# Near attention in 24-query, 32-key tiles, weights' low parts on three engines, and a new plan

## The chip, the cores and the metric

The kernel runs on one core of one Trainium2 chip. The metric is the device time of one execution in microseconds (us). The engines are TensorE (PE in the rows; its weight loads are PEld), VectorE (DVE), ScalarE (ACT), GpSimd (POOL) and SyncE (SP), which starts most transfers. Each engine works through its own list of instructions in a fixed order and waits on semaphores for what the others produce.

## The reference, cut to what matters

Three layers follow one another; q, k and v are 4 x 8 x 576 x 64 (batch, head, position, dimension).

```python
def _attn_ref(q, k, v):                        # factor = 4, Sd = 144, scale = 1/8
    q_d = q.reshape(B, H, Sd, factor, D).mean(axis=3)        # k_d, v_d alike
    ...
    out_up = np.repeat(sm_attn(q_d, k_d, v_d), factor, axis=2)      # far part
    mask = np.abs(pos[:, None] - pos[None, :]) < factor
    scores = np.where(mask, scale * np.matmul(q, k.transpose(0, 1, 3, 2)), -1e9)
    ...
    return out_up + np.matmul(attn, v)                        # near part

def _moe_ref(x, w1, w2, w3, w_out):            # x 2304 x 512, w1..w3 512 x 768
    h = np.maximum(np.maximum(x @ w1, x @ w2), x @ w3)
    return h @ w_out

def _moe2_ref(x, w_gate, w1, w2):              # 8 experts, each 512 -> 1024 -> 512
    expert_idx = np.argmax(x @ w_gate, axis=1)
    ...
        out[mask] = gate_w[mask, None] * (np.maximum(xe @ w1[e], 0.0) @ w2[e])
```

So each position attends to 144 averaged positions (far) and to the at most seven positions nearest to it (near).

## The kernel before, in words

**Attention** is worked in 16 pairs of heads, numbered u. For each pair q and k lie with two heads on 128 partitions and 576 positions along them.
- *Far part*: four neighbouring positions are summed (on VectorE by `sum4`, line 345, or on TensorE by matmuls with the identity, `tp`, line 354, which the flag "pp" chooses), scores `td` (459) are reduced, exponentiated and normalised, turned by `tu` (509), and multiplied with value sums. The value sums come from `sum4_v`, three GpSimd instructions (365 to 367).
- *Near part*: the 576 queries are cut into ten tiles of 58 queries; a tile needs 64 keys. `near` (378 to 390) puts a mask into two PSUM banks `ts` of five tiles each with matmuls (380, 382), then adds the scores with 20 matmuls per pair (389; the chip's list shows each run as two). VectorE takes the maximum per bank (399), subtracts it (405); ScalarE exponentiates; VectorE sums (433), inverts (437, 441) and normalises (445, or GpSimd with the flag "nn"). With the flag "nb" ScalarE does the subtraction and the sum by itself. Five transposes `tt` (493) into two banks turn the result, ScalarE copies it to `pt`.
- *Output*: `to` in two banks of 288 columns. A pair with the flag "pb" takes the wide way: the far part is spread over all 576 columns by six matmuls (534, run as twelve), and the near matmuls (548) add to it. The others have the far part in 144 columns, `tz` (520), and VectorE adds it to the near part while it spreads it, `x` (557). Then ScalarE rounds to a high part of `xb` (575), and VectorE or GpSimd takes the low part (577).

**The hidden layer.** Float32 products are made from high and low parts: high x high, high x low and low x high, 12 matmuls of 256 columns for one tile `hp` (929), 18 tiles and 216 matmuls for a block of 256 tokens; nine blocks. The three weight matrices come as 64-bit floating-point words in 18 blocks of 128 x 512. ScalarE takes the magnitude (702), VectorE narrows it to float32 with four instructions (`narrow`, 709 to 719), ScalarE rounds to the high part `wh` (724), GpSimd subtracts it for the low part `wl` (727). `w_out` is treated alike in 24 blocks of 128 x 128. The first block of tokens needs the outputs of the first four head pairs, and all of a block's 18 tiles need all 18 weight blocks.

**The order.** The kernel is scheduled by hand: a planner, `Plan`, holds every piece of work as a job with an engine, a cost, the jobs it waits for, the buffers it takes and gives back, and a wanted time. Among those of an engine that can start earliest, within 0.02 us, it takes the one whose wanted time is smallest:

```python
t0 = min(t for t, _ in c)
...
c = [x for x in c if x[0] <= t0 + (0.02)]
...
t, j = min(c, key=lambda x: (x[1]["want"], x[1]["n"]))
```

The wanted times come from tables of numbers (`BATCH`, `PAIR`, `STEP` for attention, `WEIGHTS`, `W_OUT`, `HIDDEN`, `ROWS`), the form of each pair from `FORMS`. Where the planner sees TensorE waiting it puts in `warm` matmuls (1835), whose result is read by nobody. PSUM has two tags of four banks: "at" for attention, "mm" for the hidden layer. The expert layer follows, planned by the same class.

Of the kernel before, what the change touches and what calls it, by code (L numbers as in the profile page):

```python
# [10 lines left out]
F32 = mybir.dt.float32  # L11
F32R = mybir.dt.float32r
# [22 lines left out]
WIN, KW = 58, 64  # L35
NW = 10
CUT = (0, S // 2, S)
NEG = -8.0e9
# [3 lines left out]
    "fn sq xl",  # L42
    "fn nn pb sk xl",
    "fn pb pp sq",
    "fn nb nn sq xl",
    "nb pb",
    "fn nn sk xl",
    "nb pb pp sk sq",
    "nb pp sq",
    "",  # L50
    "pp sq",
    "nn",
    "nn pp sq",
    "fn nn pp xl",
    "nb sk sq xl",
    "nn sk",
    "fn nb sq",
# [3 lines left out]
BATCH, PAIR, STEP = (-274.5, 218.0, 224.5, 310.0), 14.0, (38.4, -2.5, 82.2, 8.0, -10.4, 1.3, -5.5, -32.1, 50.8, -98.4)  # L61
WEIGHTS, W_OUT = (-61.6, -163.2, -24.2, -102.5, 169.6, 33.5), (-204.54, 5.46)
HIDDEN, ROWS, RESTS = (1322.17, 50.07, -176.85), (908.92, -14.66), 10.0
# [11 lines left out]
def queries(w):  # L75

    g, i = divmod(w, NW // 2)
    return g * S // 2 + i * WIN, min(WIN, S // 2 - i * WIN)


def first_key(w):

    return min(max(queries(w)[0] - 3, 0), S - KW)


def _consts():
# [18 lines left out]
    mask = np.zeros((2, 64, 3, KW))  # L105
    for i, w in enumerate((0, 1, NW - 1)):
        q = queries(w)[0] + np.arange(WIN)
        k = first_key(w) + np.arange(KW)
        mask[:, 0:WIN, i] = np.where(np.abs(q[:, None] - k[None, :]) < 4, 0.0, NEG)
# [163 lines left out]
class Attention:  # L273
# [5 lines left out]
    def __init__(s, nc, pool, psum, q, k, v, vs, C, block):  # L279
# [4 lines left out]
        s.vb = [pool.tile([128, NW // 2, 2, D], F32, name=f"vb{i}") for i in range(s.VB)]  # L284

    def setup(s):
        nc, P = s.nc, s.pool
        s.ident16 = P.tile([128, 128], BF16, name="ident16")
        nc.scalar.copy(out=s.ident16, in_=s.C["ident"])
        s.mask16 = P.tile([128, 3, KW], BF16, name="mask16")  # L290

    def plan_mask(s, pl, mask):
        st = {}

        def load():
            st["m"] = s.tile("pt", [128, NW // 2, 128]).rearrange("p a b -> p (a b)")[:, 0:3 * KW]
            s.nc.sync.dma_start(out=st["m"], in_=mask)
# [30 lines left out]
    def load_vb(s, u):  # L328
# [3 lines left out]
        s.nc.sync.dma_start(out=s.st[u]["vb"].rearrange("p i h d -> p (i h d)"), in_=s.vs[b, hp])  # L332
# [29 lines left out]
    def sum4_v(s, u):  # L362

        nc, vr = s.nc, s.st[u]["vr"]
        nc.gpsimd.tensor_tensor(out=vr[:, :, 0:2], in0=vr[:, :, 0:2], in1=vr[:, :, 2:4], op=ALU.add)
# [1578 lines left out]
```

## Time and profile before

| what | value |
|---|---|
| three runs, us | 706.24, 707.4, 709.99 (median 707.4) |
| the profiled execution, us | 710.75 |
| its span on the core, us | 708.9 |
| mean granted TensorE clock | 0.988 of full speed |
| read from and written to device memory | 75.18 MB and 9.70 MB |

The span is the time from the first to the last recorded instruction; the profiled execution is 1.85 us longer. Busy shares are means over the whole span; attention and the weights fill its first part, the hidden layer and the experts the rest, so each stretch is read by itself. An instruction's duration can include what it waits for on a shared resource, so the shortest and the mean duration of one form are read side by side.

### The profile page before, as it was taken

The page shows a single profiled execution, that of the slowest core. Times are in us where ns is not written, and L with a number is a line of the kernel's source. Part 1 is how long each engine was busy: PE and PEld are TensorE (multiplying, and loading weights), DVE is VectorE, ACT ScalarE, POOL GpSimd, SP SyncE. Part 2 cuts the span into 40 slices and gives each one's busy share as a digit, 9 for nine tenths or more (in the row PEclk, how much of TensorE's full clock was granted, in tenths as well). Part 3 has the DMA queues.
Part 4 walks back from the last instruction along what each step waited for, and adds up shares of the span by engine and source line. Part 5 has one row for each costly group of instructions (what it writes and reads, how often), then busy time and mean ns, then how long its engine had stood idle before and what let it go on. Part 6 is the DMA issues. An engine that isn't in the chain of part 4 may idle for free. (4 is left out here: it accounts for less than half of the span.)

```text
span 708.9 us, 15595 instructions
## 1 busy us (share of the span) xinstructions
PE 684.8 (97%) x6145; PEld 605.4 (85%) x6155; DVE 359.6 (51%) x900; ACT 270.4 (38%) x781; POOL 167.5 (24%) x197
## 2 busy tenths in 40 slices
PE   9989799999999999999999999999999999999993
PEld 5655689889899999999999999889888788787772
DVE  3999998988543552242222228377121121148860
ACT  3655564666441552231111112341222222156850
POOL 3656664433630121110000000213211210201110
PEclk9999999999999999999999999999999999999997
DMA  8447442335330110101000001624534342535440
GB/s 287 140 152 249 153 137 78 109 116 159 115 122 13 33 52 5 44 1 48 17 16 16 16 31 58 202 91 153 183 113 156 132 136 90 187 126 172 169 142 28
DMA packets 34547, 75.24 MB, mean 106 GB/s; under 512 B 4575, under 2 KB 7903, under 8 KB 34464
## 3 DMA queue, kind: packets, MB, share of 16 engines
q1 hardware_dynamic: 28832, 59.73, 26.0%
q0 software_dynamic: 3040, 9.70, 4.2%
q10 hardware_dynamic: 2592, 4.72, 1.8%
q8 instruction: 50, 0.82, 0.5%
q14 instruction: 33, 0.27, 0.1%
HBM read 75.18 MB, written 9.70 MB: 120 GB/s over the span
## 5 line engine op out<-in xcount | busy, mean ns | idle before, releaser
L929 PE MATMUL hp<-xb,wh 128*128 128x256 f32 x1296 | 228.6, 280 | 0.1
L929 PEld LDWEIGHTS hp<-xb,wh 128*128 128x128 f32 x1296 | 196.8, 189 | 1.3 <-issue 0.6
L929 PE MATMUL hp<-xb,wl 128*128 128x256 f32 x648 | 179.9, 278 | 0.0
L929 PEld LDWEIGHTS hp<-xb,wl 128*128 128x128 f32 x648 | 122.1, 188 | 0.0
L939 DVE TENSOR_TENSOR hf<-hf,hp 128x256 f32<-128x256 f32 x108 | 45.2, 419 | 90.7 <-PE hp L929 88.4
L1499 PEld LDWEIGHTS ehp<-xT,ew 128*128 128x128 f32 x672 | 78.3, 188 | 3.6 <-ACT ob L1657 1.7
L1499 PE MATMUL ehp<-xT,ew 128*128 128x256 f32 x672 | 79.9, 280 | 0.0
L1513 DVE SCALAR_TENSOR_TENSOR ehT<-ehp,ehT 128x256 fp32r<-128x256 f32 x56 | 23.7, 424 | 107.4 <-ACT ehT L1511 107.3
L1523 PE MATMUL eo<-ew,ehT 128*128 128x512 f32 x336 | 78.2, 392 | 0.0
L1523 PEld LDWEIGHTS eo<-ew,ehT 128*128 128x128 f32 x336 | 62.5, 188 | 15.3 <-DVE xT L1598 0.8
L957 PE MATMUL yp<-woh,ht 128*128 128x260 f32 (+1 forms) x408 | 70.5, 292 | 0.0
L942 ACT CAST ht<-hf 128x256 fp32r<-128x256 f32 x54 | 21.9, 406 | 105.9 <-DVE hf L939 105.7
L1577 POOL DMA_INDIRECT xg<-y,r_go x14 | 14.5, 1036 | 187.3 <-DVE r_go L1115 120.7
L957 PEld LDWEIGHTS yp<-woh,ht 128*128 128x128 f32 x408 | 56.9, 188 | 1.8 <-issue 0.8
L1662 POOL DMA_INDIRECT out_dram<-ob,r_si x19 | 20.1, 1059 | 122.2 <-ACT ob L1657 102.9
L1568 DVE TENSOR_TENSOR ew<-wr,ew 128x1024 fp32r<-128x1024 f32 x36 | 42.9, 1221 | 11.6 <-ACT ew L1564 10.6
L1511 ACT ACTIVATE ehT<-ehp 128x256 fp32r<-128x256 f32 x56 | 21.5, 383 | 67.5 <-PE ehp L1499 67.4
L957 PE MATMUL yp<-wol,ht 128*128 128x260 f32 (+1 forms) x204 | 43.2, 288 | 0.0
L1564 ACT CAST ew<-wr 128x1024 fp32r<-128x1024 f32 x36 | 37.0, 1052 | 6.8 <-PE ehp L1607 2.6
L1835 PE MATMUL warm<-const-bfloat16-1.0 128*128 128x512 bf16 x123 | 33.1, 417 | 1.9 <-issue 0.8
L1657 ACT ACTIVATE ob<-eo,r_ga 128x512 f32<-128x512 f32 (+1 forms) x18 | 12.1, 676 | 58.7 <-PE eo L1523 29.4
L727 POOL TENSOR_TENSOR wl<-tmp,wh 128x512 fp32r<-128x512 f32 x18 | 27.4, 1524 | 24.7 <-ACT wh L724 24.6
(230 smaller groups left out, 1034.3 us busy)
## 6 DMA issues: line engine op xcount, KB each, us to landing
wr<-in_moe_w_dram SPq DMA_DIRECT2D x36, 512.0 KB
rw<-in_moe_w_dram SPq DMA_DIRECT2D x64, 256.0 KB
raw<-in_moe_w_dram SPq DMA_DIRECT2D x18, 512.0 KB
vb<-in_vs_dram SPq DMA_DIRECT2D x16, 320.0 KB
vr<-in_v_dram SPq DMA_DIRECT2D x16, 288.0 KB
qt<-in_q_dram SPq DMA_DIRECT2D x16, 288.0 KB
kt<-in_k_dram SPq DMA_DIRECT2D x16, 288.0 KB
y<-ys ACTq DMA_DIRECT2D x18, 256.0 KB
```

Of the source, the lines that this page charges most:

```text
L727: s.nc.gpsimd.tensor_tensor(out=lo, in0=t, in1=hi.bitcast(F32), op=ALU.subtract)
L929: s.nc.tensor.matmul(t, s.w[a][:, kk, g, m * 128:(m + 1) * 128], s.xb[j][:, x, kk], start=n == 0, stop=n == 11)
L939: s.nc.vector.tensor_tensor(out=s.hf[j, m], in0=s.hf[j, m], in1=s.hp.pop((j, m, g)), op=ALU.max)
L942: s.nc.scalar.copy(out=s.ht[j][:, 0, m], in_=s.hf[j, m])
L957: s.nc.tensor.matmul(p, s.ht[j][:, a, kk, ts], s.wo[w][:, kk, c0:c1], start=kk + i == 0, stop=kk + i == 7)
L1499: s.nc.tensor.matmul(t, s.W1[j][:, a, f * 128:(f + 1) * 128], s.xL[:, x, j], start=n == 0, stop=n == 11,)
L1511: nc.scalar.activation(out=h, in_=t, func=ACTF.Relu)
L1513: nc.vector.scalar_tensor_tensor(out=l, in0=t, scalar=0.0, in1=h.bitcast(F32), op0=ALU.max, op1=ALU.subtract,)
L1523: s.nc.tensor.matmul(s.op[k, 0], h[a][:, j, i * 128:(i + 1) * 128], s.W2[:, b, j], start=j == 0 and w == 0, stop=j == 7 and w == 2,)
L1564: s.nc.scalar.copy(out=h, in_=r)
L1568: (s.nc.gpsimd if eng == "Pool" else s.nc.vector).tensor_tensor(out=l, in0=r, in1=h.bitcast(F32), op=ALU.subtract)
L1835: nc.tensor.matmul(t, one(128), one(512), start=True, stop=True)
```

## The change

- **Near tiles.** 24 queries and 32 keys in place of 58 and 64. The positions are cut into four parts (`NP`) of six tiles. All scores of a pair stand in one bank of 128 x 3 x 4 x 32; they take 48 matmuls per pair (run as 96). One maximum, one subtraction and one sum for a pair, each over 384 columns; three transposes into one bank. The mask has three variants of 32 keys. Value rows for the near part grow from 320 to 384 KB per pair, as more tiles overlap.
- **Outputs.** Four banks of 144 columns in place of two of 288, taken by turns from the tags "at" and "mm"; 48 near matmuls of 24 columns (run as 96). `x` and `xb` come in four pieces in place of two.
- **Low parts of the weights.** A table, `LOW`, puts each on GpSimd, VectorE or TensorE: of 18 blocks nine, five and four, of the 24 of `w_out` eight, twelve and four. On TensorE the value times the identity, less the high part times the identity, go into a bank, and ScalarE copies it out.
- **Value sums.** A new flag "dv" puts the value sums on VectorE, in nine pairs of 16.
- **The plan.** New costs for the jobs (a `tp` job 2.08 in place of 0.99), new forms and new wanted times. Pairs that take the wide way: four before, five now; pairs that sum q and k on TensorE: six and six.

Lines have other numbers now: scores 393, maximum 403, subtraction 408, sum 435, transposes 494, outputs 538 and 550, `x` 559, `xb` 577 and 579, narrowing 707 to 717, low parts 725, 761 and 762, `hp` 942, `warm` 1849.

```diff
-WIN, KW = 58, 64
-NW = 10
-CUT = (0, S // 2, S)
+WIN, KW = 24, 32
+NP = 4
+NW = S // NP // WIN
+CUT = range(0, S + 1, S // NP)
...
 FORMS = (
-    "fn sq xl",
-    "fn nn pb sk xl",
...
+    "dv pb pp sq xl",
+    "fn nb nn sq",
...
+LOW = (
+    "Pool", "PE", "DVE", "PE", "Pool", "Pool",
...
-WEIGHTS, W_OUT = (-61.6, -163.2, -24.2, -102.5, 169.6, 33.5), (-204.54, 5.46)
+WEIGHTS, W_OUT = (-206.2, 90.3, 239.1, 628.7, 412.7, 434.6), (-1970.43, 64.68)
...
+        t = st["ts"] = s.bank([128, NW // 2, NP, KW], "ts")
+        x, n = t.rearrange("p a i k -> p (a i) k"), NW // 2 * NP
+        for i, (a, b) in enumerate(((0, 1), (1, n - 1), (n - 1, n))):
+            m = s.mask16[:, i:i + 1].to_broadcast([128, b - a, KW])
+            nc.tensor.matmul(x[:, a:b], s.ident16, m, start=i == 0, stop=False)
+        for w in range(0, NW, 2):
+            for i in range(NP):
+                for p in range(2):
+                    k, c = first_key(i, w + p), CUT[i] + (w + p) * WIN
+                    for h in range(2):
+                        r, o = slice(64 * h, 64 * h + 64), 64 * p + 32 * h
+                        nc.tensor.matmul(
+                            t[o:o + WIN, w // 2, i], st["q"][r, c:c + WIN], st["k"][r, k:k + KW],
+                            start=False, stop=w == NW - 2 and i == NP - 1,
+                        )
...
+    def out_bank(s, i):
+        return s.psum.tile([128, S // NP], F32, name="to", tag=("at", "mm")[i % 2], bufs=4)
...
+        for t in range(NW):
+            for i in range(NP):
                 for h in range(2):
-                    p = 64 * (h ^ g)
+                    r, c = slice(32 * i, 32 * i + 32), t % 2 * 64 + 32 * h
                     nc.tensor.matmul(
...
+                        st["to", i][64 * h:64 * h + 64, t * WIN:t * WIN + WIN], st["vb"][r, t, h],
+                        st["pt"][r, t // 2, c:c + WIN], start=alone, stop=alone or t == NW - 1,
...
-        add("sv", "Pool", 2.5, lambda: s.sum4_v(u), "lr", t=T[2])
+        sv = "DVE" if "dv" in flags else "Pool"
+        add("sv", sv, 1.25 if sv == "DVE" else 2.5, lambda: s.sum4_v(u, sv), "lr", t=T[2])
...
+        def less():
+            n = int(np.prod(st["v"].shape[1:]))
+            p = st["p"] = s.bank(n, "wlow")
+            s.nc.tensor.matmul(p, s.C["ident"], st["v"], start=True, stop=False)
+            s.nc.tensor.matmul(p, s.nid, hi(), start=False, stop=True)
+            vals.append(st["v"])
+
+        j = pl.add("PE", d[5], less, [j, more], want, get=("mm",), put=(tag + "t",))
+        return pl.add("ACT", d[6], lambda: s.nc.scalar.copy(
```

How instructions stand now, at three places. First VectorE (DVE), the start of its list before, where `qk` are sums of four, `smx` and `sm` the near part, `dmx` the far part:

```order
L345 TENSOR_REDUCE qk<-qt 128x144
L345 TENSOR_REDUCE qk<-kt 128x144
L399 TENSOR_REDUCE smx<-ts 128x5 x2
L468 TENSOR_REDUCE dmx<-td 72x2 x2
L472 TENSOR_SCALAR dmx<-dmx 72x2
L405 TENSOR_TENSOR sm<-ts,smx 128x5x64
```

The same start now, where `tmp` is a weight block being narrowed:

```order
L403 TENSOR_REDUCE smx<-ts 128x12
L408 TENSOR_TENSOR sm<-ts,smx 128x384
L707 TENSOR_SCALAR tmp<-tmp 128x512
L709 TENSOR_SCALAR tmp<-tmp 128x512
L435 TENSOR_REDUCE sms<-sm 128x12
L713 SCALAR_TENSOR_TENSOR tmp<-raw,tmp 128x512
L439 TENSOR_SCALAR sms<-sms 128x12
```

Sums of four have left the start of the list, and the weights stand third. Next VectorE around the two `x` instructions of the fourth head pair, before:

```order
L709 TENSOR_SCALAR tmp<-tmp 128x512
L437 TENSOR_SCALAR sms<-sms 128x10
L711 TENSOR_SCALAR tmp<-tmp 128x512
L441 RECIPROCAL sms<-sms 128x10
L715 SCALAR_TENSOR_TENSOR tmp<-raw,tmp 128x512
L557 TENSOR_TENSOR x<-to,dn 128x288 x2
```

Now, with that pair's `x` in a group of three and one more:

```order
L471 TENSOR_REDUCE dmx<-td 72x2 x2
L403 TENSOR_REDUCE smx<-ts 128x12
L408 TENSOR_TENSOR sm<-ts,smx 128x384
L709 TENSOR_SCALAR tmp<-tmp 128x512
L435 TENSOR_REDUCE sms<-sm 128x12
L559 TENSOR_TENSOR x<-to,dn 128x144 x3
L713 SCALAR_TENSOR_TENSOR tmp<-raw,tmp 128x512
L707 TENSOR_SCALAR tmp<-tmp 128x512
L471 TENSOR_REDUCE dmx<-td 72x2
L559 TENSOR_TENSOR x<-to,dn 128x144
```

Between the conversion steps the near part stands in single instructions for 12 tile rows (`smx` 128x12), and `x` in pieces of 144. Last, TensorE (PE) ahead of the first hidden matmul (`hp`), before, where `warm` rows between are left out:

```order
L520 MATMUL tz<-pd,vr 128x144 x3
L354 MATMUL tp<-qt,cs 128x144 x4
L354 MATMUL tp<-kt,cs 128x144 x4
L509 MATMUL tu<-cs,ds 96x72 x6
L459 MATMUL td<-qk 72x144 x4
L1835 LDWEIGHTS const-bfloat16-1.0
L1835 MATMUL warm<-const-bfloat16-1.0 128x512
...
L389 MATMUL ts<-kt,qt 58x64 x16
L389 MATMUL ts<-kt,qt 56x64 x4
L929 MATMUL hp<-xb,wh 128x256 x2
```

Now:

```order
L393 MATMUL ts<-kt,qt 24x32 x48
L761 MATMUL wlow<-tmp,cs 128x512
L762 MATMUL wlow<-wh,nid 128x512
L1849 LDWEIGHTS const-bfloat16-1.0
L1849 MATMUL warm<-const-bfloat16-1.0 128x512
L519 MATMUL tz<-pd,vr 128x144 x3
...
L550 MATMUL to<-pt,vb_79 64x24 x48
...
L462 MATMUL td<-qk 72x144 x4
...
L942 MATMUL hp<-xb,wh 128x256 x2
```

In the lists the pieces of attention ahead of `hp` are of the same kinds; the `warm` rows ahead of it number 114 before and 50 now, and the low part of a weight block (`wlow`) stands among them.

## Rows read from the trace of the kernel before

**Rows 1.** Page, part 1: busy time, share of the span, instructions
```profile
PE 684.8 (97%) x6145; PEld 605.4 (85%) x6155; DVE 359.6 (51%) x900; ACT 270.4 (38%) x781; POOL 167.5 (24%) x197
```

**Rows 2.** Windows: stretch; its us; busy us (instructions) by engine; granted clock; DMA share; GB/s
```profile
0.00:72.00 72.00, 65.53 (x661) 41.60 (x669) 56.56 (x125) 37.90 (x137) 40.17 (x48) 0.98 0.62 205
75.00:117.00 42.00, 38.93 (x390) 35.42 (x391) 37.76 (x81) 21.50 (x71) 23.20 (x19) 0.96 0.41 125
117.00:290.00 173.00, 171.82 (x2097) 162.87 (x2096) 104.28 (x345) 84.26 (x327) 54.24 (x78) 1.00 0.27 81
88.20:91.60 3.40, 3.40 (x51) 2.88 (x51) 3.40 (x13) 3.24 (x12) 2.40 (x3) 0.50 0.35 86
```

**Rows 3.** Groups on PE, 0 to 75: count, busy us, mean ns, idle before
```profile
L1835 PE MATMUL warm<-const-bfloat16-1.0 128*128 128x512 bf16 x106 | 28.9, 423 | 1.8 <-issue 0.8 <-PEq L1931 0.8 <-DVE sm L405 0.2
```

**Rows 4.** Timeline of PE: start us, us, work [idle before, releaser]
```profile
74.86 0.50 PE L929 MATMUL hp<-xb,wh 128*128 128x256 f32 x2
...
87.09 0.74 PE L493 MATMUL tt<-cs,sm 128*128 128x128 f32 x5 [2.72 <-DVE sm L445]
```

**Rows 5.** Groups on DVE, 0 to 72
```profile
L715 DVE SCALAR_TENSOR_TENSOR tmp<-raw,tmp 128x512 int32<-128x512 int32 x10 | 9.2, 915 | 0.1
L719 DVE SCALAR_TENSOR_TENSOR tmp<-raw,tmp 128x512 int32<-128x512 int32 x10 | 8.9, 887 | 0.1
L709 DVE TENSOR_SCALAR tmp<-tmp 128x512 f32<-128x512 f32 x10 | 7.1, 710 | 1.3 <-ACT tmp L702 1.1
L711 DVE TENSOR_SCALAR tmp<-tmp 128x512 int32<-128x512 int32 x10 | 5.4, 538 | 0.0
L399 DVE TENSOR_REDUCE smx<-ts 128x5 f32<-128x320 f32 x10 | 4.6, 480 | 0.8 <-PE ts L389 0.8
...
L433 DVE TENSOR_REDUCE sms<-sm 128x10 f32<-128x640 f32 x3 | 2.4, 812 | 0.1
...
L345 DVE TENSOR_REDUCE qk<-qt 128x144 f32<-128x576 f32 x3 | 2.2, 728 | 8.2 <-DMA qt<-in_q_dram 8.2
...
L577 DVE TENSOR_TENSOR xb<-to,xb 128x256 fp32r<-128x256 f32 (+3 forms) x8 | 1.9, 300 | 1.6 <-ACT xb L575 1.6
L557 DVE TENSOR_TENSOR x<-to,dn 128x288 f32<-128x288 f32 x4 | 1.6, 445 | 0.0
```

**Rows 6.** Lines 709 and 719: ns min/median/max, first and last start
```profile
L709 DVE TENSOR_SCALAR tmp<-tmp x18: 411/456/2285, 16.4 to 104.7; 128x512 f32<-128x512 f32 x18
...
L719 DVE SCALAR_TENSOR_TENSOR tmp<-raw,tmp x18: 675/684/1668, 30.1 to 107.1; 128x512 int32<-128x512 int32 x18
```

**Rows 7.** Groups on POOL, 0 to 72
```profile
L727 POOL TENSOR_TENSOR wl<-tmp,wh 128x512 fp32r<-128x512 f32 x9 | 13.7, 1525 | 13.6 <-ACT wh L724 13.6
L485 POOL TENSOR_TENSOR ds<-ds,dsu 72x288 f32<-72x288 f32 x8 | 6.0, 774 | 10.0 <-DVE dsu L441 9.0 <-DVE sms L437 1.0
L365 POOL TENSOR_TENSOR vr<-vr 96x384 f32<-96x384 f32 x4 | 4.4, 1092 | 5.1 <-DMA vr<-in_v_dram 4.9 <-PE ts L389 0.2
L367 POOL TENSOR_TENSOR vr<-vr,cs 96x384 f32<-96x384 f32 x4 | 3.6, 906 | 0.3
L366 POOL TENSOR_TENSOR vr<-vr 96x192 f32<-96x192 f32 x4 | 3.0, 750 | 0.3
```

**Rows 8.** Timeline of PE, pieces of attention between other work
```profile
74.14 0.79 PE L389 MATMUL ts<-kt,qt 64*58 64x64 f32 x40
...
92.28 3.07 PE L534 MATMUL to<-pd,vr 96*128 96x288 f32 x12
...
95.29 0.81 PE L548 MATMUL to<-pt,vb 64*64 64x58 f32 x40
...
99.24 0.71 PE L493 MATMUL tt<-cs,sm 128*128 128x128 f32 x5
```

**Rows 9.** Windows of line 389 alone, within its piece at 74.14
```profile
74.13:74.16 0.03, 0.02 (x4) 0.03 (x4) 1.00 1.32 546
74.16:74.23 0.07, 0.07 (x4) 0.07 (x8) 1.00 0.85 351
```

More of the change, by code (lines that the diff above doesn't have):

```diff
@@ L103, in _consts @@
     }
[L105 to L109, printed above, removed]
+    mask = np.zeros((2, 2, 32, 3, KW))
+    for n, (i, t) in enumerate(((0, 0), (0, 2), (NP - 1, NW - 2))):
+        for j in range(2):
+            q = CUT[i] + (t + j) * WIN + np.arange(WIN)
+            k = first_key(i, t + j) + np.arange(KW)
+            mask[j, :, 0:WIN, n] = np.where(np.abs(q[:, None] - k[None, :]) < 4, 0.0, NEG)
     c["mask"] = mask.reshape(128, -1)
@@ L283, in __init__ @@
         s.st = {u: {} for u in range(s.n)}
-        s.vb = [pool.tile([128, NW // 2, 2, D], F32, name=f"vb{i}") for i in range(s.VB)]
+        s.vb = [pool.tile([128, NW, 2, D], F32, name=f"vb{i}") for i in range(s.VB)]
     def setup(s):
@@ L485, in far_norm, with turn_near, take_near @@
         s.on(on).tensor_tensor(out=x, in0=x, in1=r.to_broadcast([72, 2, 3, 48]), op=ALU.mult)
-    def turn_near(s, u, g):
+    def turn_near(s, u):
         nc, st = s.nc, s.st[u]
-        a, b = ((0, 3), (3, NW // 2))[g]
-        t = st["tt", g] = s.bank([128, b - a, 128], "tt")
-        for i in range(a, b):
-            x = st["sm"][:, i].rearrange("p g k -> p (g k)")
-            nc.tensor.transpose(t[:, i - a], x, s.C["ident"])
-    def take_near(s, u, g):
+        t = st["tt"] = s.bank([128, NW // 2, 128], "tt")
+        for a in range(NW // 2):
+            nc.tensor.transpose(t[:, a], st["sm"][:, a].rearrange("p i k -> p (i k)"), s.C["ident"])
+    def take_near(s, u):
         st = s.st[u]
-        a, b = ((0, 3), (3, NW // 2))[g]
-        if g == 0:
-            st["pt"] = s.tile("pt", [128, NW // 2, 128])
-        s.nc.scalar.copy(out=st["pt"][:, a:b], in_=st.pop(("tt", g)))
+        st["pt"] = s.tile("pt", [128, NW // 2, 128])
+        s.nc.scalar.copy(out=st["pt"], in_=st.pop("tt"))
     def turn_far(s, u):
@@ L1913, in _lay @@
     given = {"q": inputs["q"].swapaxes(2, 3), "k": inputs["k"].swapaxes(2, 3)}
-    keys = np.array([first_key(w) for w in range(NW)])[:, None] + np.arange(KW)
-    v = inputs["v"].reshape(B, H // 2, 2, S, D)[:, :, :, keys].reshape(B, H // 2, 2, 2, NW // 2, KW, D)
+    keys = np.array([[first_key(i, t) for t in range(NW)] for i in range(NP)])[..., None] + np.arange(KW)
+    v = inputs["v"].reshape(B, H // 2, 2, S, D)[:, :, :, keys]
     given["vs"] = v.transpose(0, 1, 3, 5, 4, 2, 6).reshape(B, H // 2, 128, -1)
```

244 lines of the change are left out of this document (112 added, 132 removed).

## The prediction

> **What bounds the kernel now.** I read the busy shares first, then busy time by stretch, then TensorE's order of time, then the costs on VectorE and GpSimd. TensorE is busy 97% of the span [rows 1], so a plain reading says "cut matmuls". The stretches say where more is to be had. From 117 to 290 us TensorE is busy 171.8 of 173 us at the full clock; from 0 to 72 it is busy 65.5 of 72, and that flatters it [rows 2]: 28.9 us of what it did before 75 us are `warm` matmuls, fillers whose result nobody reads [rows 3]. The first hidden-layer matmul starts at 74.86 [rows 4]. Up to there TensorE has about 39 us of attention pieces (65.5 busy by 72, nearly all of the 3 us that follow, less 28.9); the rest is filling and waiting. Who holds it up? VectorE: its first input lands at 8.2 us [rows 5], and of the 63.8 from there to 72 it is busy 56.6 [rows 2]. It reduces and normalises scores, and it turns 18 weight blocks into float32 with four instructions each. So VectorE bounds the kernel up to about 75 us, in part up to 117, and TensorE's own work from there on.
>
> Behind 74.86 two smaller losses show. TensorE waits 2.72 us for a normalised tile at 87.09 [rows 4], and then the granted clock is 0.50 for 3.4 us, the level of 1.2 GHz [rows 2], which costs 1.7. With 3.1 us idle in all between 75 and 117 [rows 2] that is 4.8 us.
>
> The time is therefore three terms: when the hidden layer opens, what is lost up to 117, and TensorE's work behind the opening. The profiled execution took 710.75 us, its span 708.9; the three runs have a median of 707.4, so differences come from the profile and are applied to 707.4.
>
> **Term 1: when the hidden layer opens.** Its first matmul needs the outputs of four head pairs, and the fourth pair's `x` comes from VectorE. Ahead of it TensorE's order holds the same pieces in both kernels (six score pieces, four output pieces, three pairs of `tp`). What differs is filler: 114 `warm` matmuls before, 50 now. Taking fillers from a waiting engine is worth nothing by itself; what counts is VectorE's list up to that fourth `x`. Priced by rows of before [rows 5], other shapes at the step from 320 to 640 elements (0.48 to 0.81):
> - weights, 39 conversion instructions become 36: two fewer at 0.9, one at 0.6: -2.4
> - row maxima, 10 at 0.48 become 6 of 384 elements at 0.55: -1.5; row sums, 3 at 0.81 become 5 at 0.55: +0.3
> - sums of four queries or keys, 6 at 0.73 become 4: -1.5
> - outputs in more and smaller pieces, 4 `x` at 0.45 become 8 at 0.3, and 8 `xb` become 18 of about 0.25: +2.7
> - taken over from GpSimd, the value sums of one pair (three instructions) and one weight block's low part: +2.3. No VectorE row shows them. Bounds: 1.2 (0.3 each), and GpSimd's own 1.09, 0.75, 0.91 and 1.53 [rows 7], 4.3; I take VectorE instructions of their size
> - subtracting, normalising, the far part and small scalars together: -2
> Together -2 us.
>
> Then contention. The conversions have floors of 0.41 and 0.68 us in this trace and stretch to 2.3 and 1.7 [rows 6]. Up to 72 us their means of 0.71, 0.54, 0.92 and 0.89 lie above the floors by 8.7 us for ten blocks [rows 5]. GpSimd is busy 40.2 us in that stretch [rows 2]. Five low parts at 1.53, one set of value sums (2.75) and four normalisations at 0.77 [rows 7] leave GpSimd ahead of that point: -13.5, 26.7 remain. If stretching goes with GpSimd's busy time, 8.7 becomes 5.8: -3.
>
> Then VectorE's 7.2 us of idle time from 8.2 to 72. The new order comes to the weights with its third instruction and so has work that waits for no other part; I give it 4 us, with bounds 0 and 7.2.
>
> The sum is -9: the hidden layer opens at 66 us. Bounds: 75 if nothing of this comes, 57 if only TensorE's own order limits it (8 us to the first input, 39 of pieces, 36 further fillers at 0.27 [rows 3]).
>
> The Trainium skill, page "SBUF — State Buffer", section "SBUF: two separate sides", calls the port that VectorE and GpSimd share an exclusive lock, held for a whole instruction; VectorE instructions with two SBUF inputs meet it too. That the floors stretch up to fourfold agrees. By that rule GpSimd's 13.5 us would come off in full and not by a third, and the opening would lie near 59: rival B.
>
> **Term 2: up to 117 us.** The first block's 216 `hp` need all 18 weight blocks. In the new order TensorE reaches the last eight some 25 us behind the opening; VectorE has 19 and 17 conversions left at the fourth `x`, 20 us at their floors [rows 6], and about 10 of other work: just in time. I keep 2.8 of the 4.8 us: -2, with bounds -4.8 and +5.
>
> **Term 3: TensorE's work behind the opening.** There every us of work is one of time [rows 2].
> - Turning: 5 transposes last 0.71 with their tail [rows 8], now 3. I take 0.22 off for each of twelve pairs behind the opening: -2.6.
> - Scores: 40 matmuls take 0.72 (74.14 to 74.86) [rows 4, 8], ten sets of four: four start within 0.03 us, and 0.07 later there are still only these [rows 9], so four parts of the array run side by side. Now there are 96 (48 in the order, run as two each, as 20 were run as 40) of half the columns. Half a set's time, 24 x 0.036, is 0.86; starting at the rate of those four is 96 x 0.0075 = 0.72; I take 0.8, and the mask's matmuls are 0.1 shorter: 0 for ten pieces, bounds -0.2 and +1.0 each.
> - Outputs: 40 take 0.81 with their tail, the scores 0.79 [rows 8]; 96 of 24 columns: 0, same bounds.
> - A fifth pair goes the wide way, 3.01 us (92.28 to 95.29) [rows 8], and not the narrow one of a quarter of the columns: +2.3.
> - Low parts on TensorE: 512 float32 columns twice at the wide way's 0.25 for 288, and half of that again: 1.1, bounds 0.5 (filler-like columns) and 1.4 (0.14 for 128, a transpose). One large and four small ones lie behind the opening: +2.3.
> Sum +2.
>
> At nothing: ScalarE's extra casts and copies, about 12 us over 290, hidden since it is busy 38 of the first 72 us [rows 2]; at worst 3 us would show ahead of the opening. Value loads grow from 320 to 384 KB, 1 MB in all, while loads wait for free buffers. Each output takes four banks where it took two, two of them from the hidden layer's four; a bank is drained in under 0.5 us, so I price that at 0; at worst a piece of 1.2 us is lost for each of twelve pairs, +14.
>
> Total -9 - 2 + 2 = -9: 701.7 by the profiled execution, **698.4** by the median.
>
> **The rivals.**
> - A, the forecast: chance 0.50, by itself 693 to 704.
> - B, the opening comes far sooner, since GpSimd's relief counts in full or only TensorE's shortened order limits it: opening at 59, 7 us more, 691.4. For it: the stretched conversions. Against it: VectorE's plain list is only 2 us shorter. 0.20.
> - C, the gain is given back: idle time takes the fillers' place, the last weight blocks or the shared banks come late. Half of term 1 (-4.5), term 2 at +3, term 3 as it is: 708. For it: the blocks are just in time, and with 64 fewer fillers the clock may fall more often, at 1.7 each. 0.15.
> - D, slower: a small matmul has a fixed price. The pieces of 64 and of 58 columns take the same time, 0.72 for 40 or 18 ns each; if that is a price per matmul, 96 take 1.73. Ten score and twelve output pieces behind the opening give 22 x 1.0 = +22: 720.4. It decides from about 12.5 ns on, where 22 x 96 x 4.3 ns eats the 9 us. Against it: four starting within 0.03 us [rows 9]. 0.15.
>
> To D belongs a rule: the Trainium skill, "TensorEngine Tiling (Array Packing)", section "Instruction Overhead", gives each matmul some 60 cycles and warns against tiling a dimension that is small already. An estimate by it is 25 ns each and some 735 us. The trace speaks against it, since 18 ns is less.
>
> **From the cases to the numbers.** 0.5% (3.5 us) is about what a measurement of this kernel can tell from no change. Faster by more: nearly all of A, B and a little of C, 0.69. Within: C and A's edge, 0.16. Slower: D, 0.15. The range 689 to 712 leaves out the lower tail of B and most of D.
>
> **What would show it.** In the profile after: the first `hp` near 66 (above 72: term 1 failed; below 61: B); under 60 fillers ahead of it; conversions nearer to 0.41 and 0.68; a piece of 96 score matmuls of 0.7 to 0.9 us (1.4 or more: D); TensorE idle under 4 us from the opening to the last of the first 216 `hp` (more, at low parts or banks: C); the full clock from there on. The prediction is wrong if the opening doesn't move, or if the 96 matmuls cost over 1.2 us.

## The result and the profile after

| | us, median | ratio to before, 95% interval |
|---|---|---|
| before (7 runs) | 708.0 (706.2 to 710.0) | |
| after (7 runs) | 713.5 (713.2 to 716.7) | 1.0093 [1.0069, 1.0116] |

The forecast was 698.4, 9 us faster; the change made the kernel 5.5 us slower. The profiled execution of after has a span of 714.0, 5.1 more than that of before, and the account below is of these two. Executions of after differ: four took 713.2 to 713.5 us and three, the profiled one among them, 715.8 to 716.7.

The page of after: busy time of TensorE (PE), and the queue that brings its instructions (packets, MB, share of 16 engines).

```profile
PE 687.9 (96%) x7925; PEld 618.3 (87%) x7925; DVE 348.1 (49%) x952; ACT 266.2 (37%) x783; POOL 126.3 (18%) x159
...
q8 instruction: 64, 1.05, 0.6%
```

The same queue on the page of before:

```profile
q8 instruction: 50, 0.82, 0.5%
```

TensorE's matmul records rose from 6145 [rows 1] to 7925, and the 16 KB packets of this queue from 50 to 64.

The first hidden-layer matmul, by the timeline of after, and the fillers ahead of it:

```profile
63.55 0.59 PE L942 MATMUL hp<-xb,wh 128*128 128x256 f32 x2
```

```profile
L1849 PE MATMUL warm<-const-bfloat16-1.0 128*128 128x512 bf16 x49 | 14.9, 435 | 0.8 <-PEq L1945 0.8
```

It starts at 63.55, before at 74.86 [rows 4]; 28.9 us of fillers [rows 3] became 14.9. Windows of after, read as [rows 2]:

```profile
0.00:62.00 62.00, 55.70 (x1222) 40.68 (x1223) 47.14 (x127) 35.58 (x122) 27.11 (x33) 0.97 0.71 230
64.00:101.00 37.00, 37.00 (x371) 34.25 (x370) 34.71 (x87) 19.62 (x56) 13.99 (x12) 1.00 0.44 139
101.00:290.00 189.00, 182.59 (x3078) 174.44 (x3077) 104.23 (x374) 82.71 (x347) 33.22 (x58) 0.95 0.27 80
```

The reader is to see three things. From 64 to 101, where the first 216 `hp` now stand, TensorE doesn't wait at all; before, 3.1 us were idle and 1.7 lost to the clock there. The first block ends at 100.8, 16.7 us earlier. Then, from 101 to 290, it is busy 182.6 of 189 us at a mean clock of 0.95, where before it was busy 171.8 of 173 at 1.00 [rows 2]. The gain of the first 101 us is given back there.

What brought the opening forward is read from VectorE's busy time up to it. Windows up to the first `hp`, of before, of after and of scores_moved, a run told below with the same order up to there:

```profile
0.00:74.86 74.86, 68.23 (x713) 43.33 (x721) 59.38 (x130) 40.18 (x142) 43.03 (x51) 0.98 0.61 203
```

```profile
0.00:63.55 63.55, 57.25 (x1229) 41.39 (x1230) 48.69 (x131) 35.99 (x125) 28.66 (x34) 0.97 0.72 231
```

```profile
0.00:60.92 60.92, 56.03 (x1222) 40.21 (x1230) 48.80 (x131) 36.15 (x125) 30.07 (x34) 1.00 0.75 242
```

VectorE's is the third busy time in a row. It starts its first work at 8.22 us in before and at 7.33 in after. So of the 11.3 us, 0.9 is an earlier start, 10.7 is less busy time (48.69 for 59.38), and its idle time behind the first work didn't shrink (7.25 and 7.53 us). In scores_moved this idle time is 4.25 and the layer opens at 60.92.

VectorE up to 62 us, as [rows 5]; the last four rows are a low part and the value sums, for which no row of before had a VectorE price:

```profile
L713 DVE SCALAR_TENSOR_TENSOR tmp<-raw,tmp 128x512 int32<-128x512 int32 x9 | 8.2, 911 | 0.0
...
L717 DVE SCALAR_TENSOR_TENSOR tmp<-raw,tmp 128x512 int32<-128x512 int32 x8 | 5.5, 685 | 0.0
...
L707 DVE TENSOR_SCALAR tmp<-tmp 128x512 f32<-128x512 f32 x10 | 4.4, 444 | 0.1
...
L709 DVE TENSOR_SCALAR tmp<-tmp 128x512 int32<-128x512 int32 x9 | 4.2, 472 | 0.0
...
L725 DVE TENSOR_TENSOR wl<-tmp,wh 128x512 fp32r<-128x512 f32 x1 | 0.7, 675 | 0.0
...
L371 DVE TENSOR_TENSOR vr<-vr 96x384 f32<-96x384 f32 x1 | 0.5, 519 | 0.0
...
L372 DVE TENSOR_TENSOR vr<-vr 96x192 f32<-96x192 f32 x1 | 0.4, 356 | 0.0
...
L373 DVE TENSOR_TENSOR vr<-vr,cs 96x384 f32<-96x384 f32 x1 | 0.6, 553 | 0.0
```

Lines 707, 709 and 717 (709, 711 and 719 in before) came down from 710, 538 and 887 ns [rows 5] to 444, 472 and 685; line 713 stayed. (In scores_moved the same four stand at 442, 424, 689 and 867 ns: which of them is stretched differs between executions.) Over the floors of [rows 6] they stretch by 0.33 us a block where it was 0.87.

Pieces of TensorE behind the opening: 96 score matmuls, 96 output matmuls, three transposes.

```profile
141.31 1.00 PE L393 MATMUL ts<-kt,qt 64*24 64x32 f32 x96
...
164.09 1.16 PE L550 MATMUL to<-pt,vb 32*64 32x24 f32 x96
...
165.59 0.49 PE L494 MATMUL tt<-cs,sm 128*128 128x128 f32 x3
```

With the next piece's start as the end they take 0.94, 1.08 and 0.25; before it was 0.72 for the scores [rows 4, 8], and 0.81 and 0.71 for outputs and five transposes, tails included [rows 8], 0.74 for the outputs by the next piece's start; so taken, five transposes had a mean of 0.54, and three have 0.28. The score pieces are not all like this one. The group of all score matmuls from 101 to 300:

```profile
L393 PE MATMUL ts<-kt,qt 64*24 64x32 f32 x864 | 9.7, 193 | 5.1 <-issue 5.1
```

9.7 us busy, and 5.1 us idle just before some of them, with no releaser but "issue": nothing that the profile shows was waited for. One of the places, by the timeline:

```profile
210.00 0.88 PE L393 MATMUL ts<-kt,qt 64*24 64x32 f32 x81
213.32 0.36 PE L393 MATMUL ts<-kt,qt 64*24 64x32 f32 x15 [2.45 <-issue]
```

81 of the 96 run, TensorE stands still for 2.45 us, and 15 follow. The clock, in three stretches (windows, as [rows 2]):

```profile
152.00:158.80 6.80, 6.80 (x120) 6.33 (x119) 4.41 (x19) 2.91 (x10) 0.53 (x1) 0.50 0.32 107
172.50:179.30 6.80, 6.80 (x32) 6.80 (x32) 3.94 (x12) 1.29 (x4) 1.00 (x1) 0.50 0.44 140
213.40:216.80 3.40, 3.40 (x31) 3.10 (x32) 1.80 (x4) 0.52 (x1) 0.67 (x1) 0.51 0.03 8
```

Before had one such stretch behind its opening, of 3.4 us [rows 2]; here 17.0 us run at 0.50, the level of 1.2 GHz. If all of it ran at half speed, that costs 8.5 us (1.7 in before); set form by form against the same matmuls at the full clock, it is some 7.3 (1.4).

So the 5.1 us more are made of these: opening -11.3; waits of TensorE behind it 7.5 instead of 5.2, +2.3; low clock 8.5 instead of 1.7, +6.8; work behind it +7.3. The last is the rest of the difference, and up to 1 us more of it if the low clock is counted form by form; by pieces it is scores 10 x 0.22, outputs 12 x 0.34, one more wide pair +2.9, low parts on TensorE +2.4, transposes -3.0, masks -1.0, in sum 7.6. So the smaller tiles by themselves, scores, outputs, transposes and masks, cost TensorE some 2.3 us of work there.

### The profile page after: what moved, and what is told of

The parts are those of the page before. It is cut to its first block, busy times and chain, and to the rows that moved or that the text cites. A ratio compares the mean times of both kernels' runs of the same rounds, so it can differ in the third digit from the quotient of the medians.

```text
span 714.0 us, 19155 instructions
## 1 busy us (share of the span) xinstructions
PE 687.9 (96%) x7925; PEld 618.3 (87%) x7925; DVE 348.1 (49%) x952; ACT 266.2 (37%) x783; POOL 126.3 (18%) x159
## 5 line engine op out<-in xcount | busy, mean ns | idle before, releaser
L1526 DVE SCALAR_TENSOR_TENSOR ehT<-ehp,ehT 128x256 fp32r<-128x256 f32 x56 | 23.7, 424 | 107.4 <-ACT ehT L1524 106.4
L970 PEld LDWEIGHTS yp<-woh,ht 128*128 128x128 f32 x408 | 58.5, 194 | 1.3 <-issue 0.4
L1581 DVE TENSOR_TENSOR ew<-wr,ew 128x1024 fp32r<-128x1024 f32 x36 | 42.9, 1222 | 11.6 <-ACT ew L1577 10.7
L1670 ACT ACTIVATE ob<-eo,r_ga 128x512 f32<-128x512 f32 (+1 forms) x18 | 12.1, 676 | 59.0 <-PE eo L1536 29.4
L970 PEld LDWEIGHTS yp<-wol,ht 128*128 128x128 f32 x204 | 32.5, 192 | 0.5
L988 DVE COPY lg<-yp 128x8 f32<-128x8 f32 x16 | 2.7, 166 | 60.6 <-ACT ys L979 60.6
```

The lines of the kernel that those rows point to most:

```text
L970: s.nc.tensor.matmul(p, s.ht[j][:, a, kk, ts], s.wo[w][:, kk, c0:c1], start=kk + i == 0, stop=kk + i == 7)
L1526: nc.vector.scalar_tensor_tensor(out=l, in0=t, scalar=0.0, in1=h.bitcast(F32), op0=ALU.max, op1=ALU.subtract,)
L1581: (s.nc.gpsimd if eng == "Pool" else s.nc.vector).tensor_tensor(out=l, in0=r, in1=h.bitcast(F32), op=ALU.subtract)
```

## The experiments

Theories: **S**, small matmuls come in runs of 192 instructions that outrun the supply of instructions, and stalls and low clock follow; **T**, these waits come from transfers or data; **C**, a small matmul costs by its columns; **D** of the prediction, a fixed price; later **L**, the loss is in the tiles and the rest of the change gains. What the trace of after says for S is read from two things: the instruction queue's own packets, and a count of all of TensorE's records (matmuls, weight loads and the waits of its sequencer) up to each stop. The table is worked out from the trace, times in us; the packet named is the last one that landed before the matmuls go on, and the last column counts the packets that landed before that one:

```
score matmuls stop   packet landed   they go on   after the landing   records so far   packets before
      19.05              18.02          19.33           1.31                705               1
      31.26              33.31          34.73           1.42               1217               3
     170.06             170.43         171.88           1.45               6081              22
     208.43             208.00         209.22           1.22               7105              26
     210.87             211.84         213.32           1.48               7361              27
```

Every stop ends 1.2 to 1.5 us after a packet of this queue, and stands at the same place in the count: 449 records, and 256 more for each packet before. In none of the twelve traces is TensorE ever ahead of that line, if a packet counts from 1.2 us behind its landing; after reaches it at these five places alone, and before never (370 at most). The 3.47 us at 31.26 lie ahead of the opening. The Trainium skill, "Runtime: NRT & Kernel Launch", section "Instruction fetch mechanics", says that instructions come in blocks of 256 and that fetching is hidden because they are issued more slowly than they arrive. The blocks of 256 the trace bears out; that fetching is hidden it does not, in these runs of 192 instructions in 0.94 us.

**scores_moved.** Three score pieces moved in the list, with the jobs that hang on them; the rest in place.

```diff
-BUSY, HALF = 0.6, 1.7
+BUSY, HALF, MOVES = 0.6, 1.7, ((11, 3), (13, 3), (12, 1))
...
-        for j in pl.run():
+        order = pl.run()
+        for u, n in MOVES:
+            order = later(order, u, n, pl.first)
...
+        for j in order:
             j["fn"]()
```

> The changed kernel with three score pieces (pairs 11, 12 and 13) moved behind the next three, one and three long pieces of TensorE in its list; nothing else differs. Theory S (supply of instructions): a piece of 96 matmuls and 96 weight loads, 192 instructions in about 1 us, eats the stock that TensorE has fetched (queue 8, 16 KB a time); two such pieces close together run it dry. Then the stalls at 170.1 (1.82 us), 208.4 (0.79) and 210.9 (2.45) go, and the two falls of the granted clock right behind them (172 and 213, 5.1 us lost) with them: -10 us, 704 by the profile, at least -5. Rival T (transfers): TensorE waits there for data or for the memory that the loads of q and k keep busy, whatever its own list: stalls of some 5 us stay or shift, no change within 0.3%. Rival P (price): only the price per small matmul counts: no change.

711.6 us, ratio 1.0046 [1.0024, 1.0067]; span 707.7. The scores' group from 120 to 215 (`later` puts a pair's scores behind the next n long pieces of TensorE):

```profile
L436 PE MATMUL ts<-kt,qt 64*24 64x32 f32 x480 | 5.2, 192 | 0.1
```

No wait with "issue" is left behind the opening (0.1 in all), and the low stretches at 172 and 213 are gone; one at 149.7 stays, as at 152 in after. T is out, by this and by the count above. But the gain is 2 us in the median (3.3 by the ratios), not the 5 at least that S expected. (Between the two profiled executions it is 6.3, of which 2.6 is the opening at 60.92: with the same order ahead of it, the stop of 3.47 us at 31.26 didn't come in this execution.) One reason is that the move put the exponential of these scores ahead of the copy that frees a bank for the hidden layer on ScalarE, and TensorE waits for that:

```profile
212.77 0.50 PE L986 MATMUL hp<-xb,wh 128*128 128x256 f32 x2 [2.07 <-ACT hf L993]
```

The stall went, another wait of 2.07 came.

**half_scores.**

```diff
-            for i in range(NP):
+            for i in range(0, NP, 2):
                 for p in range(2):
...
-                            start=False, stop=w == NW - 2 and i == NP - 1,
+                            start=False, stop=w == NW - 2 and i == NP - 2,
```

> The changed kernel with its order, but 24 of the 48 near-score matmuls of each pair left out (two of the four parts have the mask alone). Theory S: the piece falls from 0.94 to 0.47 us (10 behind the opening: -4.7), the stalls of 5.1 us behind the opening go as only 96 instructions stand in a piece, and most of the 8.5 us lost to the low clock too: -10 to -18, 696 to 704. Rival T: -4.7 from the pieces, stalls stay: 709. Rival P with the price in each matmul and nothing else: -4.7.

703.8 us, ratio 0.9924 [0.9898, 0.9951], 9.7 less than after. The group behind the opening:

```profile
L393 PE MATMUL ts<-kt,qt 64*24 64x32 f32 x480 | 6.1, 192 | 0.0
```

Half the matmuls take away the stalls of this line altogether, and two of three low stretches. This is what S says and more than the 4.7 us of the pieces alone. One stop of 2.76 us is left ahead of the opening, at 31.9, in a piece of 96 output matmuls.

**half_keys** and **half_queries**, the columns that stream and the columns of weights halved, every instruction kept.

```diff
-    t[o:o + WIN, w // 2, i], st["q"][r, c:c + WIN], st["k"][r, k:k + KW],
+    t[o:o + WIN, w // 2, i, 0:KW // 2], st["q"][r, c:c + WIN], st["k"][r, k:k + KW // 2],
```

```diff
+    t[o:o + WIN // 2, w // 2, i], st["q"][r, c:c + WIN // 2], st["k"][r, k:k + KW],
```

> The changed kernel with its order and all its instructions, but each near-score matmul takes 16 of its 32 keys (the other 16 have the mask alone). Theory S: the undisturbed piece stays at 0.94 us, since 96 matmuls at 9.8 ns are a price for each and not for its columns; stalls and low clock stay: within 0.3% of the changed kernel (714). Rival C (columns): the piece falls to 0.5, -4.4 us behind the opening, 709.

> The changed kernel with its order and all its instructions, but each near-score matmul has 12 of its 24 queries, so half the weight columns to load (the other half of the queries has the mask alone). From four pieces (64x24 weights 9.8 ns, 32x64 11.2, 64x58 15.6, 64x64 17.0 for each matmul) the price is about 5.5 ns and 2.8 ns more for each 1000 weight elements: the undisturbed piece falls from 0.94 to 0.73 us, -2 us behind the opening, and stalls of 'issue' stay: 708 to 713. Rival (one price for each small matmul, whatever its size): 0.94 stays, and the time within 0.3% of the changed kernel.

717.1 us, ratio 1.0113 [1.0086, 1.0140], and 716.1, 1.0128 [1.0096, 1.0160]: neither is faster than after (half_keys lies 0.5% over it by the medians and 0.2% by the ratios, where S expected 0.3% at most; half_queries lies over the 708 to 713 expected), and three stalls and three low stretches stand where they stood, within 3 us. An undisturbed piece, first with half the keys, then with half the queries:

```profile
140.28 0.97 PE L393 MATMUL ts<-kt,qt 64*24 64x16 f32 x96
```

```profile
142.82 0.98 PE L393 MATMUL ts<-kt,qt 64*12 64x32 f32 x96
```

Up to the next piece they take 0.90 and 0.91, against 0.94. C is out, and so is my law of weight elements, which expected 0.73.

**split_before.** The kernel before, each near matmul cut in two.

```diff
-                    nc.tensor.matmul(
-                        t[o:o + z, i], st["q"][r:r + 64, c:c + z], st["k"][r:r + 64, k:k + KW],
+                    for e in (0, KW // 2):
+                        nc.tensor.matmul(
+                            t[o:o + z, i, e:e + KW // 2], st["q"][r:r + 64, c:c + z],
...
```

> The kernel before with its order and its columns, but every near-score matmul cut into two of 32 keys and every near-output matmul into two of 29 or 28 columns: 80 and 80 in place of 40 and 40 as the chip runs them. Theory S: at 9.8 and 11.2 ns each a score piece goes from 0.72 to 0.78 and an output piece from 0.74 to 0.90; behind the opening (10 and 12 of them) +2.5 us, and stalls where pieces stand next to each other (163, 171, 187 to 199, 249 to 264), 2 to 8 us with the clock that falls behind them: 712 to 719 by the profile. Rival C (columns decide): no change within 0.3%. Rival D of the prediction (18 ns for each): 1.44 a piece, +15 us, 723.

724.9 us, ratio 1.0227 [1.0200, 1.0254], over S's 712 to 719. Of the stalls that S expected one of 0.91 us came behind the opening, at 169.6, and no low clock; the opening came 4.3 us later. A score piece and an output piece:

```profile
148.80 1.32 PE L390 MATMUL ts<-kt,qt 64*58 64x32 f32 x80
...
136.16 1.43 PE L550 MATMUL to<-pt,vb 64*64 64x29 f32 x80
```

1.25 and 1.36 us up to the next piece: 15.6 and 17.0 ns for each, near D's 18, though the columns are the same as before. S expected the prices of after (9.8 and 11.2) and is wrong in that: the price belongs to the form. A matmul with 64 rows and 58 or 64 weight columns costs 15.6 to 18.5 ns, one with 64 rows and 12 or 24 columns or with 32 rows and 64 columns 9.4 to 11.3. The columns that stream count little: halved, they took off 8 to 13% in the large form (18 to 15.6 and 18.5 to 17.0) and 4% in the small one. Why the form sets the price is not shown.

**pool_same_order.** After's order, all low parts on GpSimd.

```diff
-        (s.nc.vector if on == "DVE" else s.nc.gpsimd).tensor_tensor(out=lo, in0=t, in1=hi.bitcast(F32), op=ALU.subtract)
+        s.nc.gpsimd.tensor_tensor(out=lo, in0=t, in1=hi.bitcast(F32), op=ALU.subtract)
...
-            s.nc.tensor.matmul(p, s.C["ident"], st["v"], start=True, stop=False)
-            s.nc.tensor.matmul(p, s.nid, hi(), start=False, stop=True)
+            s.low(st["v"], hi(), lo(), "Pool")
...
+        return pl.add("ACT", d[6], lambda: None, [j], want, put=("mm",))
```

> The changed kernel with its order, but every weight block's low part on GpSimd again: the 24 matmuls and 8 copies of the TensorE way are left out, the 17 subtractions of VectorE go to GpSimd at their place in the order. If the low parts on TensorE cost what the prediction says, TensorE has 2.4 us less behind the opening; if GpSimd's work stretches VectorE's conversions, these grow again (0.44 to 0.5 or more for line 707, 0.68 to 0.8 for line 717) and the opening comes 1 to 3 us later, and the 216 matmuls of the first block end 0 to 4 us later for blocks that wait for GpSimd. Sum -2 to +5 on the changed kernel's 713.5, most likely +1. Rival: the opening came forward by the low parts that left GpSimd: without that it comes at 70 or later, and the time is 718 or more.

712.9 us, ratio 1.0056 [1.0022, 1.0090], as after. The first `hp`, and the window from 120 to 290:

```profile
69.05 0.59 PE L937 MATMUL hp<-xb,wh 128*128 128x256 f32 x2
```

```profile
120.00:290.00 170.00, 165.74 (x2808) 158.08 (x2807) 94.25 (x322) 73.74 (x313) 39.45 (x69) 1.00 0.26 78
```

The opening comes 5.5 us later, but little of that is seen to come from the low parts. The conversions did not grow as expected: 437, 553, 811 and 730 ns, 2.53 us a block where after had 2.51. VectorE is about as busy up to the opening (49.2 us for 48.7) and idle longer (11.8 for 7.5). The stop of scores at 35.6 is 1.0 us longer, and a wide piece fell into a stretch at 0.50 of the clock (23.7 to 30.6), 5.89 us where the same piece took 3.21 in after. One stretched instruction beside a low part on GpSimd is found, the first value sum, 1.53 us where it took 0.52 in after. The two wide pieces, here and in after, and that sum:

```profile
25.03 5.89 PE L538 MATMUL to<-pd,vr 96*128 96x144 f32 x24
```

```profile
22.32 3.21 PE L538 MATMUL to<-pd,vr 96*128 96x144 f32 x24
```

```profile
18.58 1.53 DVE L371 TENSOR_TENSOR vr<-vr 96x384 f32<-96x384 f32 x1
```

So that the opening hangs on the low parts, as the rival said, is shown for about 1 us; its 70 and 718 did not come. The time stays, since no low stretch lies behind the opening here (17 us of it lie ahead). With the same order at 150 us the clock did not fall: where it falls is not settled by the order of pieces alone. And an instruction other than a small matmul can be the one that waits: at 210.7, right behind scores, an `hp` matmul stops for 1.39 us at the same line of the count.

**spread.** As scores_moved, with what hangs on the moved pieces moved on all engines, and one `tp` piece too.

```diff
+MOVES = ((('tk', 12), 1), (('n', 11), 3), (('n', 12), 1), (('n', 13), 4))
```

> The changed kernel with four pieces of TensorE moved in its list, what hangs on them moved with them on the other engines: the scores of pairs 11, 12 and 13 behind three, one and four long pieces of the hidden layer or its output, and the sum of the keys of pair 12 (tp) behind one, so that it no longer stands with the sum of the queries and the gate's weights in a row of light work. Theory S, with the clock as its second half: no wait of scores with the releaser 'issue' behind the opening (5.1 us before), no fall of the granted clock at 172 and 213 (5.1 us lost), nor at 152 (3.4): 701 to 706 by the profile against 714.0, the ratio 0.990 to 1.000 to the kernel before. Rival (the fall at 152 has another cause, as a busy TensorE stands ahead of it): it stays, 704 to 709.

714.6 us, ratio 1.0081 [1.0056, 1.0106]: a miss. The scores behind the opening, and the window from 120 to 290:

```profile
L440 PE MATMUL ts<-kt,qt 64*24 64x32 f32 x960 | 10.3, 192 | 0.4 <-issue 0.4
```

```profile
120.00:290.00 170.00, 165.33 (x2691) 158.19 (x2690) 90.20 (x310) 70.44 (x304) 32.15 (x55) 0.98 0.24 73
```

"issue" is down from 5.1 to 0.4 and the low clock behind the opening from 8.5 to 3.4, but the opening came at 65.3, behind a stall of 3.2 us at 32.7 that was left where it was, and seven new waits of 0.2 to 1.0 us stand behind the opening. At 172.0 the clock still fell for 3.4 us, with no "issue" ahead of it but a wait of 0.68 us for ScalarE that ended at 170.0. Moving pieces by hand in a list that was planned with other costs shifts the waits.

**small_replanned, large_replanned, large_replanned2.** The list planned again, with costs that the traces show; the first with after's tiles, the others with before's tiles and the rest of the change. Two places of the first:

```diff
-        add("n", "PE", 1.1, lambda: s.near(u), "lq", "lk", s.masked, get=("at", "sm"), act=1.1)
+        add("n", "PE", 1.22, lambda: s.near(u), "lq", "lk", s.masked, get=("at", "sm"), act=0.5)
...
-            "on", "PE", 0.76, lambda: s.out_near(u), "cn", "lb", *(["of"] if one else []), t=T[7],
+            "on", "PE", 1.08, lambda: s.out_near(u), "cn", "lb", *(["of"] if one else []), t=T[7], act=0.3,
```

> The changed kernel with job costs taken from its own trace (scores 1.22 and outputs 1.08 us a pair, counted as light work of TensorE), and tables, low parts and forms of its own, made so that pieces of 192 instructions stand apart; four pairs take the wide way. Theory L: the price of the small tiles stays (+6 us behind the opening against the kernel before), but stalls of 'issue' and the low clock behind the opening shrink from 13.6 us to under 6, the opening stays at 61 to 66: 702 to 709. Rival (nothing of it can be planned away): 711 to 716.

> The tiles of the kernel before (58 queries, 64 keys, two banks, outputs in two halves) with the rest of the change (low parts of the weights on three engines by a table, value sums on VectorE by a flag), job costs taken from the traces, and tables of forms and wanted times of its own. Theory L: the loss of the change is in the small tiles (their price on TensorE, their instructions and what follows them), its gain in the rest. Then the opening comes at 62 to 69 us, TensorE's work behind it is that of before (627 us of 634 without waits and low clock), waits and low clock take 3 to 8: 695 to 704 by the profile, the ratio 0.980 to 0.993. Rival O: the early opening came from the small tiles' shorter list on VectorE; with large tiles it stays at 72 to 75, and the time at 704 to 711.

> As large_replanned with another set of tables and forms, to tell what the tiles do from what one order does. Theory L: 695 to 704 again, within 4 us of the other. Rival: the order decides more than the tiles, and the two lie more than 6 us apart.

| | us | ratio to before | opening | waits and low clock behind it |
|---|---|---|---|---|
| small_replanned | 698.7 | 0.985 [0.982, 0.988] | 73.7 | 2.6 and 0 |
| large_replanned | 695.0 | 0.980 [0.977, 0.983] | 75.0 | 1.4 and 0 |
| large_replanned2 | 695.6 | 0.981 [0.978, 0.984] | 68.5 | 2.3 and 0 |

All three beat both kernels. The two large ones lie 0.6 us apart, as expected. small_replanned missed what was expected of it twice, 698.7 under the 702 to 709 and an opening at 73.7 behind the 61 to 66. In small_replanned the near matmuls from 64 us on (one score piece and one output piece of them stand ahead of the opening):

```profile
L393 PE MATMUL ts<-kt,qt 64*24 64x32 f32 x960 | 10.2, 193 | 0.0
...
L550 PE MATMUL to<-pt,vb 32*64 32x24 f32 x1152 | 13.8, 219 | 0.0
```

The same prices (193 and 219 ns in the pipe; the scores had 193 in after), and no idle time ahead of them. (Ahead of the opening two stops are left, 1.99 us in scores at 28.4 and 1.15 in fillers at 49.3, at the same line of the count.) Windows from 101 to 290, first of small_replanned, then of large_replanned:

```profile
101.00:290.00 189.00, 188.71 (x3203) 181.82 (x3203) 110.10 (x390) 87.13 (x377) 36.36 (x62) 1.00 0.27 80
```

```profile
101.00:290.00 189.00, 188.06 (x2305) 179.84 (x2304) 115.75 (x377) 90.79 (x373) 49.95 (x73) 1.00 0.26 77
```

188.7 and 188.1 of 189 us at the full clock, where after had 182.6 at 0.95. So stalls and low clock can be planned away with these tiles. But that is not all that the new plan did, since it chose other forms too. From after to small_replanned the profiled span falls by 16.5 us: waits and low clock behind the opening take 13.4 off and an opening 10.1 us later puts them on again; the sums of four on TensorE, of which after has 48 matmuls behind its opening and small_replanned none, take 12.1 off.

Nor are the 3.7 us between 698.7 and 695.0 the price of the tiles: behind the opening small_replanned has two wide pairs and large_replanned none. The wide matmuls of small_replanned behind the opening:

```profile
L538 PE MATMUL to<-pd,vr 96*128 96x144 f32 x48 | 6.2, 286 | 0.0
```

Theory L's early opening did not come in large_replanned (75.0, as rival O said), yet the time did: TensorE's work behind the opening is shorter. The sums of four on TensorE, behind the opening of before, and all of them in large_replanned:

```profile
L354 PE MATMUL tp<-qt,cs 128*128 128x144 f32 x24 | 6.7, 437 | 0.0
L354 PE MATMUL tp<-kt,cs 128*128 128x144 f32 x24 | 6.7, 435 | 0.0
```

```profile
L363 PE MATMUL tp<-kt,cs 128*128 128x144 f32 x16 | 4.6, 445 | 0.0
L363 PE MATMUL tp<-qt,cs 128*128 128x144 f32 x16 | 4.5, 441 | 2.1 <-DMA qt<-in_q_dram 2.1
```

Before has 48 behind the opening, 12.2 us up to the next pieces; large_replanned has 32 in all, ahead of it. The plan of before held a piece of eight at 0.99 us; it takes 2.04. The two wide pairs behind the opening of before are gone too, 6.0 us, for 1.7 more in the narrow way. These two savings, 16.5 us, are as large as the whole gain (16.4 by the spans), and come from the forms that the plan chose. (Waits and low clock fell by 5.5 as well, and other work behind the opening grew by about as much.) No run plans the kernel before anew without low parts on three engines and value sums on VectorE, so that the rest of the change gains, as theory L says, is not shown.

## Why the prediction was wrong, step by step

- **What bounds the kernel.** Right: the opening, the stretch up to 117 and TensorE's work behind are where the time went. But an opening is worth what it is only while the same pieces stand ahead of it; large_replanned opens where before does and is 14 us faster. Neither of the two signs that the prediction named for being wrong came: the opening moved, and the 96 matmuls cost 0.94 and 1.08 us.
- **Term 1**, opening at 66, -9: it came at 63.55, -11.3. That is near in sum and not in its parts, so in part luck. VectorE's busy time was to fall by 5 (its list -2, contention -3) and fell by 10.7; the 4 us of idle time that the new order was to save were not saved in after (7.53 us for 7.25), with a stop of TensorE of 3.47 us for want of instructions among what it waited for. The conversions stretched 5.4 us less in ten blocks where -3 was taken. A low part and a set of value sums on VectorE took 0.68 and 1.43, together 2.1 of the 2.3 priced. That the conversions stretched less because of GpSimd's low parts is not shown: in pool_same_order they did not grow again. Rival B's opening at 59 did not come; its 13.5 us could not come off in full, as the stretch they were to shorten was 8.7. (That stretch goes up to 5.6 times the floor by [rows 6], not fourfold.)
- **Term 2**, -2: all 4.8 us were gained up to the end of the first block; the last weight blocks and the shared banks came in time, and rival C's places for a loss were empty.
- **Term 3**, +2: here the forecast failed. *Scores: 0* and *Outputs: 0* were mis-sized: a score piece +0.22, less the 0.1 for the mask that was priced with it, and an output piece +0.34, +5.3 in all. I took the matmuls to cost by the columns that four side by side stream; half_keys shows that halving the columns takes only 4% off. Wide pair (+2.9 for 2.3) and low parts (+2.4 for 2.3) were about right; transposes gave -3.0 for -2.6.
- **The full clock from there on**, and "TensorE's work behind the opening" as busy time without waits: the larger miss. Behind 101 us waits and low clock took 13.9 us more than behind 117 in before (5.4 and 8.5); less the 4.8 of term 2, that is the +9.1 above. Nothing in the working counted instructions. It priced 96 matmuls where 40 were, but not that 192 instructions in 1 us, in pieces close together, are more than their queue brings: 5.1 us of "issue", shown by the count at the stops, by scores_moved and by half_scores to be made by the number and nearness of these pieces. The low clock's 8.5 us were priced at nothing too, and what brings the low clock about stays open.
- **The rivals.** The result lies between C and D. D's mechanism, a price for each, holds with 9.8 and 11.2 ns and not 18; with the measured opening and work alone (-11.3 and +7.3) the kernel would have gained 4 us. C's "the clock may fall more often, at 1.7 each" came true behind the opening, five times 3.4 us in place of one, but not for C's reason: the fillers that are gone stood ahead of the opening, where the clock fell once for 3.4 us in both kernels. The rule of some 60 cycles for a matmul (the Trainium skill, "TensorEngine Tiling (Array Packing)", "Instruction Overhead") gave 25 ns and stays too high here, but its advice, not to tile what is small already, fits these tiles, whose scores and outputs got dearer by 0.22 and 0.34 us a piece.

What stays open is what the clock's falls hang on. The one at 152 us came in after, half_keys, half_queries, half_scores and, later or earlier, in the two kernels with moved pieces, and did not in pool_same_order with the same order of pieces. Nor is it shown that the stops bring the falls at 172 and 213 about, as S took them to: in scores_moved and half_scores the two went together, but in spread the clock fell at 172.0 without such a stop, and in pool_same_order stops of 0.62 and 1.39 us at 207 to 212 brought no fall.

## What to carry to other kernels

Before a matmul is cut into smaller ones, count instructions: read a piece's price per matmul at the nearest form, and ask how many instructions then stand in a microsecond. Idle time of TensorE with the releaser "issue" in the middle of a run of small matmuls is a sign that its instructions came late; count its records up to such places, and if they lie a whole number of blocks apart, set these pieces apart. Give the planner the durations that the trace shows: a plan with measured costs, and with the forms and tables that came of it, took the same tiles from 713.5 to 698.7.

## What was not expected of the hardware

- A small matmul's price hardly moves when the columns streamed or the weight columns are halved (0.94, 0.90 and 0.91 us for 96), but goes from 9.8 to 15.6 ns when its weights reach from 24 to 58 columns, 32 columns streaming in both.
- TensorE can run out of instructions in straight code: they come in packets of 16 KB, 256 records to a packet, and after stood still for 0.3 to 3.5 us, each time at 449 records and a multiple of 256, until 1.2 to 1.5 us after a packet had landed. The kernel before, with 80 instructions in a piece, came no nearer than 370.
